# A delta-rule attention and MoE kernel: key-state and query-state products joined into one with 64 stationary columns, with the keys of the first four chunks loaded alone

## The chip, the core and the metric

The kernel runs on one core of a Trainium2 chip. The core has a matrix engine (TensorE, in the profile PE, with its weight loads on a row of their own, PEld), a vector engine (VectorE, DVE), an activation engine (ScalarE, ACT), a general engine (GpSimd, POOL), a queue that mostly starts transfers (SyncE, SP), and 16 DMA engines. The metric is device time in microseconds (us) of one execution. Less is better.

## What is computed

The reference has two parts. The first is a recurrence over 768 positions for each of 4 x 8 heads with a state of 48 x 48; the second is a feed-forward layer over all 3072 tokens.

```python
k_n = k / (np.linalg.norm(k, axis=-1, keepdims=True) + 1e-06)
for t in range(S):
    kt, vt, bt = (k_n[:, :, t], v[:, :, t], beta[:, :, t, None])
    y[:, :, t] = np.einsum('bhd,bhde->bhe', q[:, :, t], state)
    v_old = np.einsum('bhde,bhd->bhe', state, kt)
    state = state + bt[:, :, :, None] * np.einsum('bhd,bhe->bhde', kt, vt - v_old)
...
h = x @ w_in
g = h - np.tanh(h)
return (g @ w_out).astype(np.float32)
```

Here x is y with the 8 heads side by side (3072 x 384); w_in is 384 x 2048 and w_out 2048 x 384, both handed over as float64 words that the kernel turns into pairs of 32-bit numbers itself.

## The kernel before

**The recurrence in chunks.** The 768 positions are cut into 24 chunks of 32, and four chunks make a group. All 32 (batch, head) pairs of a chunk are worked on together: the batch picks a quarter of the 128 partitions, the head a stretch of columns. For a chunk s the steps are:

- `score` (L438 to L474): key-key and key-query products, 32 small matmuls with 32 stationary columns and 64 moving ones (L456). VectorE or ScalarE copies the first half into `gs` (L465, L468), ScalarE the second into `pq` (L472), and GpSimd masks `pq` (L478).
- `solve` (L483 to L605): once in a group, VectorE turns the four chunks' `gs` into the inverse of a triangular matrix for each pair: a transpose (L501), the norms (L511 to L549), 30 steps of two operations each (L577, L579), and a last transpose into `tt` (L588). The solve of group 0 is on the way of everything behind it.
- `prep` (L644 to L651): the values are multiplied by the key norms, on VectorE for the first four chunks and on GpSimd later.
- `chain` (L658 to L734): on TensorE the key-state product (L672), on VectorE its subtraction from the values (L679), on TensorE the query-state product (L689), the solve product with `tt` (L704), the state's new part (L719) after ScalarE has copied `u_sb` (L711), and the part of the output that comes from the chunk itself (L729), on top of L689 in the same PSUM bank. VectorE adds the new part to the state (L745). Each of these products is 32 small matmuls, and the next chunk's key-state product needs the new state.
- `output` (L749 to L772): ScalarE copies the output (L754), TensorE transposes it (L764), ScalarE and VectorE make a high and a low part of it in `xt` (L768, L770).

**The feed-forward layer.** The weights are decoded in 16 pieces (`decode`, `piece`, L779 to L846): ScalarE takes them apart, VectorE joins the bits (L823), ScalarE rounds to the high part (L826), and the low part comes from TensorE for the first `SPARE` pieces (L832, L833, with a copy by ScalarE, L836) and from VectorE for the rest (L841). Six windows of 512 tokens each then meet 16 slices of the hidden layer: `hidden` (L875, 9 matmuls of 512 columns for a unit), `gate` (ScalarE L892 and L900, VectorE L894 and L902), `out_units` (L925, 9 matmuls). In window 0 the first `F0` slices are done in two halves of 256 columns.

**What sets the order.** `Plan` (L86 to L230) is a list scheduler with made-up costs. It runs when the program is built and fixes one order for each engine; on the chip each engine takes its instructions in that order and waits where an operand is missing. Due times, the table `QUIRK` and constants such as `OPEN` and `F0` steer it. `warm` (L342 to L357) gives TensorE filler matmuls (L356) on zeros wherever the planner sees it idle before the last window; on the chip they are run whether or not TensorE would have been idle. The order of the first transfers is the list `FIRST`, and all are on SP's queue, which issues one after the other and holds the rest back while one waits.

**PSUM.** Two banks (`psa`) serve scores, key-state, solve, new state and transposes in turn; one (`psy`) holds the output; two (`ph`) the hidden units and three (`po`) the accumulation of the layer's output. `Ring` objects make a step wait until a bank is read out.

Of the kernel before, what the change touches and what calls it, by code (L numbers as in the profile page):

```python
# [14 lines left out]
ALU = mybir.AluOpType  # L15
PSUM = bass.MemoryType.PSUM
# [3 lines left out]
C = 32  # L20
# [65 lines left out]
class Plan:  # L86
# [3 lines left out]
    SLACK = {"PE": 0.211, "DVE": 14.4, "ACT": 0.344, "POOL": 0.2, "SP": 0.0}  # L90
# [168 lines left out]
def kernel(ctx: ExitStack, tc: tile.TileContext, kq, vk, beta, w_in, w_out, const, out):  # L259
# [7 lines left out]
    ps_y = pool("ps_y", 1, space=PSUM)  # L267
    ps_h = pool("ps_h", 2, space=PSUM)
# [7 lines left out]
    cs = cst.tile([128, 193], F32, name="cs")  # L276
    ident = cs[:, 0:128]
    strict, lower = (cs[:, None, a:a + C].broadcast_to([128, H, C]) for a in (128, 161))
# [9 lines left out]
    ra, ry, rh, ro = Ring(2), Ring(1), Ring(2), Ring(1)  # L288
    held = [ps_a.tile([128, 512], F32, name=f"psa{k}") for k in range(2)]
    new = {"psa": (ps_a, ra), "psy": (ps_y, ry), "ph": (ps_h, rh)}  # L290

    def bank(name):
        p, r = new[name]
        e = r.take()
        return held[r.free.index(e)] if name == "psa" else p.tile([128, 512], F32, name=name), e
# [5 lines left out]
    def transfer(end, kb):  # L301
        a = max(dma[0], end + 1.5)
        dma[0] = a + kb * 1024e-3 / (370.0 if a > 45.0 else 270.0 if kb == 448 else 350.0)
        plan.moves.append((a, dma[0]))
        return Event(dma[0] + 0.4)
# [6 lines left out]
    def opening():  # L312
# [9 lines left out]
        for t in held:  # L322
            nc.vector.memset(t[32:64, :DM], 0.0)
        zeroed.t = plan.free["DVE"]

    def burn():
        ps = ps_y.tile([128, 512], F32, name="psy")
        n = BURN
        while n:
            m = min(n, 16)  # L330
            n -= m
            yield Op("PE", 0.03 * m, (), 0.0, "tiny", 4 * m)
            for i in range(m):
                rows = quad[i % 4]
# [7 lines left out]
    def warm():  # L342
        ps = ps_o.tile([128, T], F32, name="po0")
        count = lambda w: NF + F0 if w == 0 else NF
        usable = lambda: 0.0 if not pos or xt_in[NS - 1].t is not None or any(ended.get(w, 0) < count(w) for w in pos) else None
        while xt_in[NS - 1].t is None and plan.free["PE"] < 2000.0:
# [5 lines left out]
            if (BURN or gram) and len(gram) < 4:  # L352
# [9 lines left out]
    def load_keys(s, table, tag):  # L362
        kc = ld.tile([128, 2, 16, C], F32, tag=tag, name=f"{tag}{s}", bufs={"kc": KCS, "kd": KDS}[tag])
        nc.sync.dma_start(kc, kq[s].rearrange("x p u c -> p x u c"))
# [698 lines left out]
```

## Time and profile before

| | |
|---|---|
| median of three runs | 617.2 us (616.09 to 617.62) |
| the profiled execution | 617.75 us, of which the span is 615.7 us |
| busy share: PE, DVE, ACT, POOL | 97%, 62%, 36%, 7% |
| TensorE filler matmuls (L356) | 166, busy for 40.9 us |
| VectorE operations with PSUM or the state (L679, L745) | 545 ns and 550 ns each |
| moved by DMA | 51.54 MB |

The span runs from the first to the last instruction; the time of an execution is about 2 us longer. A row of the timeline has the start and the length of a run of equal instructions in us, the engine, the line, what is written and read, the shapes, and the number of instructions; idle time ahead of it stands in brackets with what ended it. A 32-bit matmul of a small product is two instructions in the trace (x64 for 32), while the rows of the built order count it once. Since matmuls are pipelined, what one costs is read from the start of a row to the start of the next, not from its length.

### The profile page before, as it was taken

What the parts mean: (1) busy time and instruction counts of PE and PEld (TensorE: products, weight loads), DVE (VectorE), ACT (ScalarE), POOL (GpSimd) and SP (SyncE); (2) the same over time, 40 slices, a digit from 0 to 9 for tenths busy, and PEclk for the clock granted to TensorE, in tenths of its full rate; (3) what the DMA queues carried; (4) which work ended last, traced back from release to release, by engine and by line L of the source; (5) the groups of instructions that cost most, each with busy time, mean ns of one, the idle gap of its engine ahead of it and who ended that gap; (6) DMA issues with size and microseconds to landing.
All of it is one profiled execution on the core that took longest, in us unless ns stands there. A gap on an engine that the chain in (4) does not pass through costs nothing.

```text
span 615.7 us, 24171 instructions
## 1 busy us (share of the span) xinstructions
PE 598.0 (97%) x11146; PEld 471.6 (77%) x11146; DVE 382.4 (62%) x831; ACT 221.5 (36%) x400; POOL 43.6 (7%) x60
## 2 busy tenths in 40 slices
PE   6999899999999999999999999999999999999996
PEld 4455688987877788788888878777888788878885
DVE  2898678886489934779625878525678632333323
ACT  2335645486422333323323233223333232242223
POOL 1110100000220001100001200001100000000000
PEclk8999899999999999999999999999999999999999
DMA  8980345212530223231123321110121000010001
GB/s 309 393 302 28 116 127 203 87 34 91 163 110 11 97 71 97 63 95 54 50 84 98 97 71 42 38 62 29 64 82 67 3 2 2 3 52 1 0 1 51
DMA packets 24500, 51.54 MB, mean 84 GB/s; under 512 B 2512, under 2 KB 2640, under 8 KB 24400
## 3 DMA queue, kind: packets, MB, share of 16 engines
q1 hardware_dynamic: 22240, 45.19, 21.8%
q10 hardware_dynamic: 2160, 4.82, 2.5%
q8 instruction: 87, 1.43, 1.0%
q14 instruction: 13, 0.11, 0.1%
HBM read 45.29 MB, written 4.72 MB: 81 GB/s over the span
## 4 chain that ended last, share of the span: by engine, by line
PE 94%; DMA 2%; DVE 1%; issue 1%; ACT 1%; SPq 0%; ACTq 0%
PE po L925 33%; PE ph L875 33%; PE po L356 6%; PE psa L456 4%; PE psa L719 3%; PE psy L729 3%; PE psa L672 3%; PE psa L704 3%; PE psy L689 3%; PE ph L832 2%; PE psa L764 1%; DMA kd<-in_kq 1%; DVE a L579 0%; PE ph L833 0%; DVE tmp L577 0%
## 5 line engine op out<-in xcount | busy, mean ns | idle before, releaser
L875 PE MATMUL ph<-xt,w 128*128 128x512 f32 (+1 forms) x918 | 215.7, 385 | 2.2 <-DVE t L894 1.0
L925 PE MATMUL po<-gh,w 128*128 128x512 f32 (+1 forms) x918 | 213.8, 383 | 0.0
L875 PEld LDWEIGHTS ph<-xt,w 128*128 128x128 f32 x918 | 164.3, 190 | 36.8 <-DVE t L894 1.4
L925 PEld LDWEIGHTS po<-gh,w 128*128 128x128 f32 x918 | 162.8, 188 | 33.6 <-DVE gh L902 1.1
L894 DVE TENSOR_TENSOR t<-ph,t 128x512 f32<-128x512 f32 (+1 forms) x102 | 66.7, 656 | 91.4 <-ACT t L892 91.0
L892 ACT ACTIVATE t<-ph 128x512 f32<-128x512 f32 (+1 forms) x102 | 58.5, 573 | 170.5 <-PE ph L875 165.0
L902 DVE TENSOR_TENSOR gh<-t,gh 128x512 fp32r<-128x512 f32 (+1 forms) x102 | 68.9, 676 | 43.0 <-ACT gh L900 41.4
L900 ACT CAST gh<-t 128x512 fp32r<-128x512 f32 (+1 forms) x102 | 60.7, 595 | 82.4 <-DVE t L894 55.1
L579 DVE TENSOR_TENSOR a<-a,tmp 128x30 f32<-128x30 f32 (+9 forms) x180 | 61.9, 344 | 5.1
L577 DVE TENSOR_TENSOR tmp<-a 128x30 f32<-128x30 f32 (+9 forms) x180 | 61.0, 339 | 4.6
L745 DVE TENSOR_TENSOR st<-st,psa 112x384 f32<-112x384 f32 x44 | 22.4, 550 | 32.1 <-PE psa L719 31.4
L356 PE MATMUL po<-wz 128*128 128x512 bf16 x166 | 40.9, 399 | 1.1 <-DVE idle L315 1.1
L478 POOL TENSOR_TENSOR pq<-pq,cs 128x256 f32<-128x256 f32 x24 | 17.9, 744 | 253.6 <-ACT pq L472 253.5
L356 PEld LDWEIGHTS <-wz 128*128 128x128 bf16 x166 | 16.3, 101 | 21.8 <-issue 4.8
L770 DVE TENSOR_TENSOR xt<-psa,xt 128x384 fp32r<-128x384 f32 x24 | 13.2, 553 | 23.7 <-ACT xt L768 23.7
L754 ACT COPY y_sb<-psy 128x384 f32<-128x384 f32 x24 | 11.5, 481 | 41.5 <-PE psy L729 41.5
L719 PEld LDWEIGHTS psa<-u_sb,v 32*48 32x48 f32 x1472 | 18.6, 119 | 8.8 <-issue 7.2
L456 PEld LDWEIGHTS psa<-kc 48*32 48x32 f32 x1344 | 20.4, 110 | 4.7 <-issue 4.2
L650 POOL TENSOR_TENSOR v<-v,nt 128x384 f32<-128x384 f32 x20 | 17.3, 874 | 93.0 <-DMA v<-in_vk 62.5
L456 PE MATMUL psa<-kc 48*32 48x64 f32 x1344 | 23.8, 222 | 0.0
L672 PE MATMUL psa<-st,kd 48*32 48x48 f32 x1472 | 20.8, 204 | 2.8 <-issue 2.8
L672 PEld LDWEIGHTS psa<-st,kd 48*32 48x32 f32 x1472 | 17.5, 107 | 7.6 <-issue 6.7
(61 smaller groups left out, 419.4 us busy)
## 6 DMA issues: line engine op xcount, KB each, us to landing
kd<-in_kq SPq DMA_DIRECT2D x23, 512.0 KB, 4.0
kc<-in_kq SPq DMA_DIRECT2D x21, 512.0 KB, 4.2
v<-in_vk SPq DMA_DIRECT2D x24, 384.0 KB, 3.6
out<-o SPq DMA_DIRECT2D x18, 256.0 KB, 2.1
raw<-in_w_in SPq DMA_DIRECT2D x5, 768.0 KB, 11.6
raw<-in_w_out SPq DMA_DIRECT2D x5, 768.0 KB, 11.2
raw<-in_w_in ACTq DMA_DIRECT2D x3, 768.0 KB, 4.8
raw<-in_w_out ACTq DMA_DIRECT2D x3, 768.0 KB, 4.3
```

What stands on the lines that cost most here:

```text
L356: nc.tensor.matmul((ps if own else pos[w][0][0]).rearrange("p (a b) -> p a b", a=4), wz, wide, start=own, stop=own, skip_group_check=not own)
L456: nc.tensor.matmul(ps[quad[b], h, :], k[:, 0], k, start=True, stop=True)
L577: nc.vector.tensor_tensor(tv, col.broadcast_to(shape), row.broadcast_to(shape), ALU.mult)
L579: nc.vector.tensor_tensor(below, below, tv, ALU.add)
L672: nc.tensor.matmul(pk[quad[b], h, :], kd[rows, 0, 2 * h + pr, :], st[rows, pr, h, :], start=True, stop=True)
L719: nc.tensor.matmul(hv(sums[b // 2][0])[HALF[b % 2], h, :], kt[rows, h, :], u_sb[rows, h, :], start=True, stop=True)
L875: nc.tensor.matmul(p, wi[f][:, a, ct, :], xt[:, b, ct, part], start=(ct == 0 and i == 0), stop=(ct == NC - 1 and i == 2))
L892: nc.scalar.activation(t_, p, AF.Tanh)
L894: nc.vector.tensor_tensor(t_, p, t_, ALU.subtract)
L900: nc.scalar.copy(gh[:, 0, :n], t_)
L902: nc.vector.tensor_tensor(gh[:, 1, :n], t_, gh[:, 0, :n].bitcast(F32), ALU.subtract)
L925: nc.tensor.matmul(po[c][:, part], wo[f][:, a, 128 * c:128 * c + 128], gh[:, b, :n], start=(f == 0 and i == 0 and z < 1), stop=(ended.get( ...
```

## The change

Six things are changed together.

1. In `chain` the key-state and the query-state product become one: keys and queries stand side by side in the loaded tile, so that 64 stationary columns go through one set of 32 matmuls (L642 of the changed kernel) into two banks `psk`. In one half of the rows the order is key, query, in the other query, key. The values `v` and keys are loaded with the same alternation, `prep` and the subtraction then work on 768 columns in place of 384 and write to a tile `wv` of their own, and the output is copied from PSUM quarter by quarter (four operations of ScalarE in place of one).
2. PSUM: `psa` is one bank in place of two, `psk` two in place of `psy`'s one. The second half of a chunk's new state goes to a bank of `ph`.
3. The keys of chunks 0 to 3 are loaded alone first (`kf`, 256 KB each) and `head` makes their key-key products; the full tiles of these chunks follow later, and `score` makes only their key-query products. The first weight transfer waits for the first `head`.
4. TensorE begins with 48 tiny matmuls on zeros (`burn`) in place of 12 fillers.
5. `SPARE` goes from 8 to 10, `F0` from 6 to 4.
6. The planner has other constants and another `QUIRK` table. The solve of group 1 may not begin before that of group 0 is done. The branch for halved solves, which was not in use, is gone.

```diff
-    SLACK = {"PE": 0.211, "DVE": 14.4, "ACT": 0.344, "POOL": 0.2, "SP": 0.0}
+    SLACK = {"PE": 0.112, "DVE": 2.784, "ACT": 0.062, "POOL": 0.2, "SP": 0.0}
...
-    ra, ry, rh, ro = Ring(2), Ring(1), Ring(2), Ring(1)
-    held = [ps_a.tile([128, 512], F32, name=f"psa{k}") for k in range(2)]
+    ra, rk, rh, ro, rwt = Ring(1), Ring(1), Ring(2), Ring(1), Ring(WS)
+    psa = ps_a.tile([128, 512], F32, name="psa")
+    two = ps_k.tile([128, 2, 512], F32, name="psk")
...
+    def load_first(s):
+        ring, tag, n = (rc, "c", CB) if s < 3 else (rlo, "lo", LB)
+        t = pre.tile([128, 2 * DM], F32 if s < 3 else I32, tag=tag, name=f"kf{s}", bufs=n)
+        t = (t if s < 3 else t.bitcast(F32))[:, :16 * C].rearrange("p (u c) -> p u c", u=16)
+        nc.sync.dma_start(t, kf[s])
...
+            if behind:
+                tc.add_manual_dep(nc.cur_bb.bb.instructions[-1], heads[0].name, SYNC, reason="keys ahead of the rest")
...
+    def head(s):
...
+        for h in range(H):
+            for b in range(4):
+                x = k[HALF[b % 2], 2 * h + b // 2]
+                nc.tensor.matmul(ps[quad[b], h, :], x, x, start=True, stop=True)
...
+        nc.vector.tensor_copy(groups[0][0][:, :, 8 * s:8 * s + 8].rearrange("p i h -> p h i"), ps)
...
-                k = kc[HALF[b % 2], :, 2 * h + b // 2, :]
-                nc.tensor.matmul(ps[quad[b], h, :], k[:, 0], k, start=True, stop=True)
+                z, u = b % 2, 2 * h + b // 2
+                k = kc[HALF[z], u]
+                nc.tensor.matmul(ps[quad[b], h, :], k[:, z], k[:, 1 - z] if g == 0 else k[:, ::-1] if z else k, start=True, stop=True)
...
-        hw.tensor_tensor(v, v, nt[:, 8 * r:8 * r + 8, None].broadcast_to([128, H, D]), ALU.mult)
+        w, wr = at.tile([128, 2, H, D], F32, name="wv", bufs=WS), rwt.take()
+        hw.tensor_tensor(w, both, nt[:, None, 8 * r:8 * r + 8, None].broadcast_to([128, 2, H, D]), ALU.mult)
...
-                        rows, pr = HALF[b % 2], b // 2
-                        nc.tensor.matmul(pk[quad[b], h, :], kd[rows, 0, 2 * h + pr, :], st[rows, pr, h, :], start=True, stop=True)
+                        z, pr = b % 2, b // 2
+                        nc.tensor.matmul(pk[64 * pr:64 * pr + 64, z, h, :], kd[HALF[z], 2 * h + pr].rearrange("p a c -> p (a c)"), st[HALF[z], pr, h, :],
+                                         start=(h == 0), stop=False, skip_group_check=True)
...
-                    nc.vector.tensor_tensor(v, v, pk, ALU.subtract)
+                    nc.vector.tensor_tensor(w, w, pk, ALU.subtract)
...
-                        nc.tensor.matmul(py[quad[b], h, :], kd[rows, 1, 2 * h + pr, :], st[rows, pr, h, :],
-                                         start=(h == 0), stop=False, skip_group_check=True)
...
-        nc.scalar.copy(y_sb, py.rearrange("p h e -> p (h e)"))
+        for b in range(4):
+            if b:
+                (_, t) = yield Op("ACT", act(DM, True), (e,), need(s) - 3.0)
+            nc.scalar.copy(yv[quad[b]], py[quad[b ^ 1], b % 2])
...
-BURN, LATCH = 0, ((9, 4), (10, 2), (16, 2))
+WS, SOLO, SLOW = 2, True, 2.0
+BURN, LATCH = 48, ((8, 1), (8, 2))
...
-WARM, HOLD, GUARD, F0 = 120.0, 90.0, 0.3, 6
-FIRST = ['k0', 'k1', 'k2', 'k3', 'b0', 'k4', 'v1', 'w4', 'v3', 'w2', 'k7', 'w0', 'k6', 'w3', 'v0', 'b1', 'v2', 'k5', 'w1']
+WARM, HOLD, GUARD, F0 = 90.0, 120.0, 0.28, 4
+FIRST = ['f0', 'f1', 'f2', 'f3', 'b0', 'w0', 'w4', 'k2', 'k1', 'v2', 'k3', 'v3', 'k0', 'w3', 'b1', 'k4', 'k6', 'w1', 'w2', 'v0', 'k7', 'v1', 'k5']
...
-LOW, SPARE, MARGIN = True, 8, 7.6
+LOW, SPARE, MARGIN = True, 10, 15.2
```

The order that the planner makes of it is shown at three places. The first is SP's queue at its start; `kc` and `kd` are full key tiles of 512 KB, `v` values of 384 KB, `raw` undecoded weights of 768 KB, `bt` beta. Before:

```order
L364 DMA kc_94<-in_kq 128x2x512
L364 DMA kd_100<-in_kq 128x2x512
L364 DMA kd_103<-in_kq 128x2x512
L364 DMA kd_106<-in_kq 128x2x512
L380 DMA bt<-in_beta 128x32
L364 DMA kc_112<-in_kq 128x2x512
L372 DMA v<-in_vk 128x768
L394 DMA raw_119<-in_w_in 128x3x512
```

In the changed kernel (its lines differ), from `kf` on to the third weight tile; the values of chunk 0 come only after four more key tiles and two more weight tiles, as the 20th transfer, and those of chunk 1 as the 22nd:

```order
L373 DMA kf0_97<-in_kf 128x512
L373 DMA kf1_115<-in_kf 128x512
L373 DMA kf2_133<-in_kf 128x512
L373 DMA kf3_147<-in_kf 128x512
L389 DMA bt_157<-in_beta 128x32
L404 DMA raw0_224<-in_w_in 128x3x512
L404 DMA raw4_226<-in_w_in 128x3x512
L364 DMA kd2_230<-in_kq 128x1024
L364 DMA kd1_232<-in_kq 128x1024
L381 DMA v_234<-in_vk 128x768
L364 DMA kd3_236<-in_kq 128x1024
L381 DMA v_238<-in_vk 128x768
```

What moved: 1 MB of keys stands ahead of the first weights where 2 MB of keys and queries stood, and the full tiles of the first chunks, which are still needed, come among weights and values.

The second place is VectorE at the end of group 0's solve. Before, the decode of weight piece 1 (`c_536`) and the norms on the values of all four chunks come behind the last transpose into `tt`:

```order
L582 TENSOR_TENSOR a_323<-a_323,gm 128x1024
L588 STREAM_TRANSPOSE tt_725<-a_323 128x32x32
L823 SCALAR_TENSOR_TENSOR c_536<-c_536,lo_582 128x768
L650 TENSOR_TENSOR v<-v,nt 128x384 x4
L823 SCALAR_TENSOR_TENSOR c_600<-c_600,lo_781 128x768
L501 STREAM_TRANSPOSE a_825<-gs_253 128x1024
```

In the changed kernel the norms on chunk 1 (`wv`, twice as wide) and the decode of piece 1 stand within the solve's steps, as do those on chunk 0, twelve rows further up and ahead of the step with 228 columns:

```order
L594 TENSOR_TENSOR tmp<-a_323 128x238
L621 TENSOR_TENSOR wv<-v,nt 128x768
L596 TENSOR_TENSOR a_323<-a_323,tmp 128x14x17
L786 SCALAR_TENSOR_TENSOR c_526<-c_526,lo_534 128x768
L594 TENSOR_TENSOR tmp<-a_323 128x234
```

What moved: three operations of 768 columns now stand ahead of `tt`, and one of them needs values that are the 20th transfer.

The third place is TensorE in the chain of chunk 13. Before (three rows of L925 with 3 matmuls each are one unit of the layer):

```order
L672 MATMUL psa_88<-st,kd_4120 32x48 x32
L689 MATMUL psy<-st,kd_4120 32x48 x32
L704 MATMUL psa_87<-v,tt_4847 32x48 x32
L925 MATMUL po_4739<-gh,w_1223 128x512 x3
L925 MATMUL po_4740<-gh,w_1223 128x512 x3
```

In the changed kernel, from the score of chunk 18 on:

```order
L500 MATMUL psa<-kc_3490 32x64 x32
L888 MATMUL po_4595<-gh,w_1451 128x512 x3
L888 MATMUL po_4596<-gh,w_1451 128x512 x3
L888 MATMUL po_4597<-gh,w_1451 128x512 x3
L729 MATMUL psa<-cs,y_sb 128x128 x3
L642 MATMUL psk<-st,kd_3964 64x48 x32
L838 MATMUL ph_89<-xt_3705,w_1286 128x512 x9
L838 MATMUL ph_90<-xt_3705,w_1604 128x512 x9
L663 MATMUL psa<-wv,tt_4578 32x48 x32
```

What moved: one product of 64 stationary columns stands where two of 32 stood, and between two users of the one bank `psa` stands a unit of the layer.

More of the change, by code (lines that the diff above doesn't have):

```diff
@@ L321, in opening @@
         nc.vector.memset(st, 0.0)
-        for t in held:
+        for t in [psa] + held:
             nc.vector.memset(t[32:64, :DM], 0.0)
@@ L326, in burn @@
     def burn():
[L327 to L334, printed above, removed]
+        ps = psa
+        for i in range(BURN // 4):
+            yield Op("PE", 0.067, (), -100.0, "tiny", 16)
+            for rows in quad:
                 nc.tensor.matmul(ps[rows, :16], wz.bitcast(F32)[rows, :32], wz.bitcast(F32)[rows, :16], start=True, stop=True)
@@ L982 @@
     for s in range(4):
[L983 removed]
+        plan.spawn(head(s))
     plan.spawn(scores())
```

322 lines of the change are left out of this document (137 added, 185 removed).

## The prediction

> **What bounds the kernel now.** I read the page first, then what TensorE waited for, then the timeline of TensorE, VectorE and DMA up to 260 us.
>
> ```profile
> span 615.7 us, 24171 instructions
> PE 598.0 (97%) x11146; PEld 471.6 (77%) x11146; DVE 382.4 (62%) x831; ACT 221.5 (36%) x400; POOL 43.6 (7%) x60
> PE 94%; DMA 2%; DVE 1%; issue 1%; ACT 1%; SPq 0%; ACTq 0%
> ```
>
> TensorE is busy for 97% of the span and holds 94% of the chain that ended last. So an instruction taken from its list shortens the run by its start-to-start time, one that is added lengthens it, and other engines count only where they make it wait. The waits of that kind, by what they follow (total, times, longest); "issue" is idle time that follows on nothing in the profile:
>
> ```profile
> PE psa L672 <- issue: 2.8, 2, 2.0
> PE psy L729 <- issue: 1.0, 1, 1.0
> ```
>
> These are the two largest of the nine rows that concern work behind the first solve product; together the nine are 7.5 us, and each of the other seven is 1.0 or less. A busy TensorE is not a useful one, though: up to that product it mostly runs fillers.
>
> ```profile
> 33.73 19.60 PE L356 MATMUL po<-wz 128*128 128x512 bf16 x90
> 53.26 0.88 PE L704 MATMUL psa<-v,tt 32*32 32x48 f32 x64
> 15.06 1.25 DVE L501 STREAM_TRANSPOSE a<-gs 128x1024 f32<-128x1024 f32 x1
> 48.97 1.96 DVE L588 STREAM_TRANSPOSE tt<-a 128x1024 f32<-128x1024 f32 x1
> ```
>
> The 90 fillers take 19.53 us, 0.217 each. Ahead of 53.26 the kernel is bound by loading the keys and by VectorE's solve, 15.06 to 50.93 us; from there TensorE's list bounds it.
>
> **Part 1: the start, 2.3 us gained.** These rows are VectorE's within and behind the solve, TensorE's second score, DMA in steps of 10 us (its rate in GB/s is the last number), and a cast of ScalarE.
>
> ```profile
> 32.23 0.40 DVE L577 TENSOR_TENSOR tmp<-a 128x228 f32<-128x228 f32 x1
> 38.45 0.40 DVE L577 TENSOR_TENSOR tmp<-a 128x234 f32<-128x234 f32 x1
> 50.78 0.94 DVE L823 SCALAR_TENSOR_TENSOR c<-c,lo 128x768 int32<-128x768 int32 x1
> 51.64 1.93 DVE L650 TENSOR_TENSOR v<-v,nt 128x384 f32<-128x384 f32 x4
> 6.39 1.07 PE L456 MATMUL psa<-kd 48*32 48x64 f32 x64
> 0.00:10.00 10.00, 7.51 (x204) 4.30 (x204) 2.78 (x7) 2.54 (x5) 1.66 (x6) 1.00 0.81 263
> 10.00:20.00 10.00, 7.63 (x141) 4.78 (x142) 5.76 (x13) 1.56 (x4) 3.42 (x4) 0.66 1.05 391
> 24.44 0.83 ACT L826 CAST w<-c 128x768 fp32r<-128x768 f32 x1 [1.02 <-DVE c L823]
> ```
>
> The second score began at 6.39, when 1 MB of keys was there; the four new key tiles are 1 MB, so the last `head` starts near 6.4, and with 0.6 for it and 0.6 for its copy the solve begins at 7.6 in place of 15.06. That lead of 7.5 us isn't kept. Ahead of the step that began at 32.23 now stands the norm on chunk 0's values, which VectorE reaches at 7.6 + 17.2 = 24.8. These values are the 20th transfer: up to and with them SP issues 9.34 MB. DMA moved 2.63 MB in the first 10 us and 3.91 in the next 10; at that rate they land at 27.2, and near 27.8 with the pause in which the first weights wait for `head`. From there: 18.7 us of the old solve (32.23 to 50.93), two norms of 768 columns and one decode, at 0.86 each by the decode's start-to-start: `tt` at 49.1.
>
> TensorE can't use all of that, because its fillers are in its list. It meets VectorE at weight piece 1, decoded 12.5 us (38.45 to 50.93) before `tt`: 36.6, and cast at 37.4. Then its order has two halves of that piece's low part, 45 fillers and two scores: 1.8 + 9.8 + 2.0 = 13.6, so the first solve product starts at 51.0 against 53.26. Bounds: 49.1 if TensorE isn't late; 53 if chunk 1's values are late too (their transfer is queued on SP behind a key tile that waits for chunk 4's score on TensorE, and VectorE's next 31 rows wait behind the norm).
>
> **Part 2: TensorE's list after that product, 9.2 us less.**
>
> ```profile
> 84.90 0.81 PE L832 MATMUL ph<-c,cs 128*128 128x384 f32 x2
> 85.81 0.93 PE L719 MATMUL psa<-u_sb,v 32*48 32x48 f32 x64
> 105.09 0.88 PE L672 MATMUL psa<-st,kd 48*32 48x48 f32 x64
> 105.91 2.41 PE L875 MATMUL ph<-xt,w 128*128 128x256 f32 x18
> 108.16 2.32 PE L925 MATMUL po<-gh,w 128*128 128x256 f32 x18
> 110.41 0.89 PE L689 MATMUL psy<-st,kd 48*32 48x48 f32 x64
> 111.22 3.50 PE L925 MATMUL po<-gh,w 128*128 128x256 f32 x27
> 119.86 4.27 PE L875 MATMUL ph<-xt,w 128*128 128x512 f32 x18
> 123.97 4.24 PE L925 MATMUL po<-gh,w 128*128 128x512 f32 x18
> 128.14 0.88 PE L704 MATMUL psa<-v,tt 32*32 32x48 f32 x64
> 206.12 1.07 PE L456 MATMUL psa<-kc 48*32 48x64 f32 x64
> 207.12 2.37 PE L875 MATMUL ph<-xt,w 128*128 128x512 f32 x9
> 217.87 0.93 PE L719 MATMUL psa<-u_sb,v 32*48 32x48 f32 x64
> 218.73 0.88 PE L729 MATMUL psy<-u_sb,pq 32*32 32x48 f32 x64
> 219.55 2.35 PE L925 MATMUL po<-gh,w 128*128 128x512 f32 x9
> 222.15 0.89 PE L672 MATMUL psa<-st,kd 48*32 48x48 f32 x64
> 222.85 0.86 PE L689 MATMUL psy<-st,kd 48*32 48x48 f32 x64
> 223.64 2.35 PE L925 MATMUL po<-gh,w 128*128 128x512 f32 x9
> ```
>
> - The two products. Side by side (17 of 23 chunks in the old order) they take 0.70 + 0.79 = 1.49; apart (6 chunks) 0.82 + 0.81 = 1.63: 35.1 in all. The joint product has 48 moving columns as they have, so it streams for as long as one; its 64 stationary columns aren't in the trace. The nearest row is L719 with 48: 0.86 against 0.82 for L729 with 32. At 0.05 for 16 columns it takes 0.82 + 0.10 = 0.92, 21.2 in all: **13.9 less**. Bounds: 0.82 (16.2 less), and 1.00 as L456, which is longer on its moving side (12.1 less).
> - Fillers: of 166, 13 stood behind the first solve product; of 148, 38 do. 25 x 0.217 = **5.4 more**.
> - Two more half pieces' low parts, 0.91 each (84.90 to 85.81), of the four more that `SPARE` brings: **1.8 more**; the other two stand ahead of the product, in part 1.
> - `F0`: four half units less and two whole ones more for each of L875 and L925. A half is 1.125, a whole 2.055 and 2.085: **0.7 less**.
> - Idle time: of the 7.5 us, the 2.0 before L672 followed on a run of small products for which instructions weren't there in time. With four products to a chunk in place of five such runs are shorter: **1.8 less** (bounds: none, or 3.8, both rows named issue).
>
> Work moved to other engines is hidden while TensorE has units to do. The rows of 384 columns that read PSUM:
>
> ```profile
> L679 DVE TENSOR_TENSOR v<-v,psa x5: 526/541/546, 209.5 to 298.6; 128x384 f32<-128x384 f32 x5
> L711 ACT COPY u_sb<-psa x4: 479/480/481, 213.7 to 266.1; 128x384 f32<-128x384 f32 x4
> ```
>
> The subtraction grows from 0.54 (the middle number, in ns) to about 0.95 us on VectorE, if it goes as the decode of 768 columns, on the chain from state to state, where the new order has a unit (2.1 us) between the joint product and the solve product. Three more copies of the output on ScalarE, 0.48 us each if 32 partitions take as long as 128, stand ahead of its transposition alone. GpSimd's norms double on an engine that is 7% busy. Without that cover the subtraction would cost 0.4 and the copies 1.4 for each chunk, 41 in all.
>
> **Sum.** -2.3 - 13.9 + 5.4 + 1.8 - 0.7 - 1.8 = -11.5 us. The profiled execution took 617.75, 0.55 above the median of 617.2; so 606.3 for it, and 606 as the median. No change means within 0.3%, 615.3 to 619.1, which is about what a measurement of this kernel can tell.
>
> **The rivals.**
>
> *More of the lead is kept.* If chunk 0's values land at 25.8, both engines are 2 us earlier, and if both waits named issue go, that is 2.0 more: 602. For it: at the 391 GB/s of the second DMA row 9.34 MB take 23.9 us, so only a quicker beginning is needed than that of the first row. Against: the pause at the first weights may be longer than 0.6 us.
>
> *The solves stay late.* VectorE has group 1's `tt` at 122.4 and TensorE needs it at 128.14:
>
> ```profile
> 120.28 2.09 DVE L588 STREAM_TRANSPOSE tt<-a 128x1024 f32<-128x1024 f32 x1
> ```
>
> From the first `tt` that is 71.5 us. VectorE's list between the two is about as long in the new order; at 71.5 it ends at 120.6, and by my count of its new rows TensorE arrives at 121 to 124. A wait of 3 us there and no gain at the start give 611.
>
> *One bank for five users.* A score is followed by two copies of ScalarE before `psa` is free:
>
> ```profile
> L468 ACT COPY gs<-psa x4: 631/643/648, 207.4 to 240.1; 128x256 f32<-128x256 f32 x4
> L472 ACT COPY pq<-psa x4: 432/437/443, 207.8 to 240.5; 128x256 f32<-128x256 f32 x4
> ```
>
> Started 0.3 after the score's end, they are done about 1.1 behind it (207.12 to 208.2). Where a unit of 2.1 stands before the next user, 1 us of delay on ScalarE is covered; where ScalarE is held up for longer TensorE waits, which two banks would have hidden. At 0.3 us a chunk that is 7, so 613; from 0.5 a chunk on nothing is left of the gain. [...]
>
> *The weight load sets the pace.* If L672's 0.70 us were the time of its 64 loads of 32 columns, 64 columns would take 1.40, and 1.51 before a unit: 23 x (1.51 - 0.92) = 13.6 more, 620, slower than before; above 1.4 us a product it eats the gain. For it: nothing in the trace has 64 columns in this packing. Against: L719's 48 columns should then take 1.05, and take 0.86. [...]
>
> That the joint product isn't joint is excluded by the order: one row of 64 columns stands where two stood.
>
> **How the numbers follow.** Main case (604 to 609) 0.60; TensorE not held 0.13; solves late 0.13; one bank 0.10, of which 0.04 at no change or worse; weight load 0.03; 0.01 for the rest. The forecast is the main case's. The range of 599 to 613 takes in the bounds of the joint product (603.7 to 607.8), of the start (604 to 608), and three rivals; outside are the dearer half of the one bank, the weight load, and gains on all terms together. Faster 0.92, same 0.03, slower 0.05.
>
> **What would show it.** Right: the joint product at 0.9 start to start; the first solve product near 51, with VectorE idle before the norm until its values land; 148 fillers; TensorE's idle time after it near 6 us, scattered. Wrong: rows in which TensorE waits for ScalarE's copies at `psa` in every chunk, a product above 1.1, or a solve product that waits for `tt` at 121.

## The result, and the profile after

The changed kernel took 611.78 us (median of 12 runs, 609.5 to 615.25), the kernel before 615.98 beside it (12 runs, 614.23 to 618.09): a ratio of 0.9927, 95% interval 0.9905 to 0.9949. It is faster and inside the range given, but outside the main case of 604 to 609: by 4.2 us and not by the 11.2 of the forecast. The profiled execution of the changed kernel took 610.21 us, 1.6 below its median, that of before 617.75, 1.8 above the median of before here; so between the two profiled executions lie 7.5 us, 7.2 of them between the spans, and the gains and losses below add up to these 7.2.

The head of the changed kernel's page: its span, the busy times, and the engines' shares of the chain that ended last.

```profile
span 608.5 us, 21905 instructions
PE 588.2 (97%) x9984; PEld 459.7 (76%) x9984; DVE 390.5 (64%) x826; ACT 257.9 (42%) x472; POOL 58.6 (10%) x60
PE 89%; DVE 4%; ACT 3%; DMA 2%; issue 2%; ACTq 0%
```

TensorE is as busy as before (97%) and still has most of the chain, but 11% of the chain is now elsewhere, where it was 6%. What TensorE waited for in the changed kernel (total, times, longest), the largest rows:

```profile
PE psa L469 <- issue: 4.4, 1, 4.4
PE ph L795 <- DVE c L786: 3.9, 1, 3.9
PE ph L469 <- issue: 2.3, 1, 2.3
PE psa L729 <- ACT y_sb L719: 1.1, 1, 1.1
```

The three largest all lie in the first 25 us. Of the rows named issue that stood behind the first solve product in the kernel before, none is left. The place of the first is seen in the list of TensorE's instructions in order of time (start, duration, line, count of records, idle time ahead):

```profile
4.60 1.07 PE L469 MATMUL ph<-kf 48*32 48x32 f32 x63
8.00 1.20 PE L469 MATMUL ph<-kf 48*32 48x32 f32 x65 [2.33 <-issue]
8.97 1.08 PE L469 MATMUL psa<-kf 48*32 48x32 f32 x62
14.44 0.31 PE L469 MATMUL psa<-kf 48*32 48x32 f32 x2 [4.39 <-issue]
24.31 0.91 PE L795 MATMUL ph<-c,cs 128*128 128x384 f32 x2 [3.91 <-DVE c L786]
50.02 7.94 PE L356 MATMUL po<-wz 128*128 128x512 bf16 x36
57.90 0.88 PE L663 MATMUL psa<-wv,tt 32*32 32x48 f32 x64
```

L469 is the product of the `head`s. The work of the third head and nearly all of the fourth was done by 10.05; then TensorE stopped for 4.39 us with two records left, out of 256. VectorE's list shows what that held up:

```profile
14.78 0.60 DVE L474 COPY gs<-psa 128x256 f32<-128x256 f32 x1 [4.92 <-PE psa L469]
15.42 1.25 DVE L538 STREAM_TRANSPOSE a<-gs 128x1024 f32<-128x1024 f32 x1
32.44 0.95 DVE L621 TENSOR_TENSOR wv<-v,nt 128x768 f32<-128x768 f32 x1
40.75 0.96 DVE L621 TENSOR_TENSOR wv<-v,nt 128x768 f32<-128x768 f32 x1 [2.22 <-DMA v<-in_vk]
54.71 1.95 DVE L604 STREAM_TRANSPOSE tt<-a 128x1024 f32<-128x1024 f32 x1
```

The solve begins at 15.42 and not at 7.6: the keys that were loaded alone and first have moved it by nothing (15.06 before). The norm on chunk 0's values (32.44) doesn't wait, since VectorE is late itself; that on chunk 1's waits 2.22 us, because their transfer stood in SP's queue behind a key tile that waited for TensorE. `tt` is ready at 56.66, and the first solve product starts at 57.90, 4.6 us *later* than before (53.26). The last 1.2 us of that are TensorE's own list, which is late too: it waited until 24.31 for a decode that stands behind the solve's first steps on VectorE, and its last 36 fillers ahead of the product start at 50.02 and are followed by it at 57.90.

Behind that product things went better. The joint product in TensorE's list, twice, with the row behind it:

```profile
231.21 1.15 PE L642 MATMUL psk<-st,kd 48*64 48x48 f32 x64
232.29 2.32 PE L888 MATMUL po<-gh,w 128*128 128x512 f32 x9
...
244.00 1.15 PE L642 MATMUL psk<-st,kd 48*64 48x48 f32 x64
245.08 2.34 PE L888 MATMUL po<-gh,w 128*128 128x512 f32 x9
```

From its start to the next row's it takes 1.08 us, not 0.92. The account of both profiles, summed over all matmul records from start to start (waits over 0.1 us apart), from the first solve product on:

| | forecast | measured |
|---|---|---|
| first solve product starts | -2.3 | +4.64 (53.26 to 57.90) |
| the two products, then the joint one | -13.9 | -11.83 (36.63 to 24.80) |
| fillers behind it | +5.4 | +6.28 (2.84 to 9.12) |
| idle time | -1.8 | -5.94 (7.53 to 1.59) |
| low parts of half pieces (L795, L796) | +1.8 | +1.71 (12.88 to 14.59) |
| units of L838 and L888 | -0.7 | -1.81 (412.94 to 411.13) |
| other small products, and the tail | 0 | -0.27 |
| sum | -11.5 | -7.22 (span 615.72 to 608.50) |

### The profile page after: what moved, and what is told of

Same layout as the page of the kernel before. It is cut to its first block, busy times and chain, and to the rows that moved or that the text cites. A ratio compares the mean times of both kernels' runs of the same rounds, so it can differ in the third digit from the quotient of the medians.

```text
span 608.5 us, 21905 instructions
## 1 busy us (share of the span) xinstructions
PE 588.2 (97%) x9984; PEld 459.7 (76%) x9984; DVE 390.5 (64%) x826; ACT 257.9 (42%) x472; POOL 58.6 (10%) x60
## 4 chain that ended last, share of the span: by engine, by line
PE 89%; DVE 4%; ACT 3%; DMA 2%; issue 2%; ACTq 0%
PE ph L838 32%; PE po L888 31%; PE po L356 4%; PE psk L642 4%; PE psa L500 4%; PE psa L663 3%; PE psk L692 3%; PE psa L679 2%; PE ph L795 2%; PE psa L729 1%; DMA raw<-in_w_in 1%; ACT y_sb L719 1%; PE ph L679 1%; DMA kc<-in_kq 1%; DVE c L786 1%
## 5 line engine op out<-in xcount | busy, mean ns | idle before, releaser
L888 PE MATMUL po<-gh,w 128*128 128x512 f32 (+1 forms) x900 | 213.7, 387 | 0.3 <-DVE gh L865 0.3
L838 PE MATMUL ph<-xt,w 128*128 128x512 f32 (+1 forms) x900 | 213.2, 387 | 0.2 <-DVE tmp L594 0.2
L888 PEld LDWEIGHTS po<-gh,w 128*128 128x128 f32 x900 | 161.7, 188 | 34.3 <-DVE gh L865 0.6
L838 PEld LDWEIGHTS ph<-xt,w 128*128 128x128 f32 x900 | 161.4, 188 | 34.1 <-DVE tmp L594 0.7
L719 ACT COPY y_sb<-psk 32x384 f32<-32x384 f32 x96 | 45.2, 471 | 37.0 <-PE psk L692 36.0
L621 POOL TENSOR_TENSOR wv<-v,nt 128x768 f32<-128x768 f32 x20 | 30.8, 1543 | 213.7 <-PE psa L663 169.3
L356 PE MATMUL po<-wz 128*128 128x512 bf16 x148 | 38.0, 393 | 0.0
L642 PEld LDWEIGHTS psk<-st,kd 48*64 48x64 f32 x1472 | 23.6, 134 | 5.2 <-issue 4.2
L642 PE MATMUL psk<-st,kd 48*64 48x48 f32 x1472 | 26.4, 220 | 0.0
L356 PEld LDWEIGHTS <-wz 128*128 128x128 bf16 x148 | 13.3, 99 | 16.6 <-issue 3.7
L651 DVE TENSOR_TENSOR wv<-wv,psk 128x768 f32<-128x768 f32 x23 | 21.9, 951 | 5.2 <-PE psk L642 4.4
L663 PEld LDWEIGHTS psa<-wv,tt 32*32 32x32 f32 x1536 | 17.9, 105 | 8.6 <-issue 5.8
L500 PEld LDWEIGHTS psa<-kc 48*32 48x32 f32 x1344 | 19.4, 107 | 5.7 <-issue 3.9
```

The source lines that it names most:

```text
L356: nc.tensor.matmul((ps if own else pos[w][0][0]).rearrange("p (a b) -> p a b", a=4), wz, wide, start=own, stop=own, skip_group_check=not own)
L500: nc.tensor.matmul(ps[quad[b], h, :], k[:, z], k[:, 1 - z] if g == 0 else k[:, ::-1] if z else k, start=True, stop=True)
L642: nc.tensor.matmul(pk[64 * pr:64 * pr + 64, z, h, :], kd[HALF[z], 2 * h + pr].rearrange("p a c -> p (a c)"), st[HALF[z], pr, h, :], start= ...
L719: nc.scalar.copy(yv[quad[b]], py[quad[b ^ 1], b % 2])
L838: nc.tensor.matmul(p, wi[f][:, a, ct, :], xt[:, b, ct, part], start=(ct == 0 and i == 0), stop=(ct == NC - 1 and i == 2))
L888: nc.tensor.matmul(po[c][:, part], wo[f][:, a, 128 * c:128 * c + 128], gh[:, b, :n], start=(f == 0 and i == 0 and z < 1), stop=(ended.get( ...
```

## The experiments

**Theory.** The gain is lost at the start, because TensorE's instructions come in blocks. The trace has a DMA queue of its own for them; its row in the DMA view of the changed kernel, from 0 to 16 us (packets, MB, share):

```profile
q8 instruction: 2, 0.03, 0.8%
```

These are two transfers of 16,384 bytes. They start at 5.65 and 12.11 us and take 0.94 and 0.99; TensorE goes on at 8.00 and at 14.44, 1.3 to 1.4 us after each has landed. It is no accident of two places: in the 14 traces of this study every wait named issue of more than 0.4 us, 33 in all, ends 1.3 to 1.6 us after a transfer of this queue has landed. Over the whole run the queue has 78 transfers, and TensorE 2 x 9,984 = 19,968 records, 256 to a transfer (the kernel before: 87 and 22,292). Between the two waits stand 65 + 62 = 127 matmul records (rows above) and as many weight loads: 254 instructions, so an estimate from these counts is 256 to a block and 64 bytes to an instruction (16,384 / 256). The places agree with it: counted over TensorE's matmul and weight-load records, those two waits stand 256 records apart, and the six of this kind in the kernel before whole multiples of 256 (the first, which ends at 12.81, and the second, at 72.25, 2,048 apart). A block of tiny products is worked off here in 2.1 us (8.00 to 10.05), and TensorE then stood still for 4.39 us ahead of the next. The 48 tiny matmuls of `burn` cost 192 instructions ahead of the heads' 512, and with them the end of a block falls two records short of the end of the fourth head. **Rival:** the heads wait for data, since keys, weights and instructions all come by DMA (queues q1 and q8 in that view).

**Experiment 1: 44 of the 48 tiny matmuls.** The planner's order is untouched; only four matmuls on zeros aren't emitted.

```diff
-            for rows in quad:
+            for rows in quad if i else ():
                 nc.tensor.matmul(ps[rows, :16], ...)
```

> [...] Theory (the last matmuls of the fourth head are just past a boundary of instruction blocks, since the tiny matmuls in front use up instructions, and wait 4.4 us for the block): the wait of 4.39 us inside the last head goes, the solve's transposition starts near 11 instead of 15.4 us, the norm then waits for chunk 0's values (31.1), the wait of 2.2 us for chunk 1's values stays or shrinks, and the first solve product starts between 54 and 56.5 instead of 57.9; 607 to 610 us where the changed kernel has 611.8, that is 1.5 to 4 us less. Rival (the four heads wait for the keys, which share the DMA engines with the rest): the last head still ends after 14 us, and nothing changes (611.8).

Measured: 605.38 us (ratio 0.9817, 0.9801 to 0.9832), 6.4 below the changed kernel. The wait in the fourth head is gone, the solve starts at 10.32, the first solve product at 53.22. TensorE's row of the fourth head is whole:

```profile
8.56 1.09 PE L469 MATMUL psa<-kf 48*32 48x32 f32 x64
```

That is more than expected, and the rival's "nothing changes" is out.

**Experiment 2: 46 and 52 tiny matmuls.** To see whether it is a threshold, the sharpest steps: two fewer, and four more.

```diff
-            for rows in quad:
+            for rows in quad if i else quad[:2]:      (46)
+            for rows in quad if i else quad + quad:   (52)
```

> The changed kernel with 46 of its 48 tiny matmuls. In its profile the last two records of the fourth head (one product of four instructions) came behind the wait, so by the theory of the instruction blocks taking 2 matmuls of four instructions away is enough: the wait inside the fourth head goes, the solve starts near 10.4, the first solve product near 53.2 to 54, and 605 to 606.5 in all. Rival (fewer tiny matmuls help because TensorE comes to the heads earlier or because something else shifts): the wait stays at 4 us and the time at 611 to 612.

> The changed kernel with 52 tiny matmuls, 4 more. By the theory of the instruction blocks about five products of the fourth head now stand behind the boundary in place of one, and wait for the same block: the wait of 4 to 4.5 us stays, the solve starts at 15 to 16 us, and the time is the changed kernel's, 610.5 to 612.5. Rival (the time grows with the number of tiny matmuls, 6.4 us for 4): 617 or so.

Measured: 604.53 us with 46 (ratio 0.9808, 0.9782 to 0.9835), 614.37 with 52 (0.9960, 0.9944 to 0.9977). TensorE's list with 46, in order of time:

```profile
4.67 1.30 PE L469 MATMUL ph<-kf 48*32 48x32 f32 x66
7.84 1.02 PE L469 MATMUL ph<-kf 48*32 48x32 f32 x60 [1.87 <-issue]
...
8.68 1.08 PE L469 MATMUL psa<-kf 48*32 48x32 f32 x62
...
14.56 1.08 PE L500 MATMUL psa<-kd 48*32 48x32 f32 x64 [4.25 <-DVE z L565]
...
52.84 0.88 PE L663 MATMUL psa<-wv,tt 32*32 32x48 f32 x64
```

The 4.25 us ahead of the score (L500) is a wait for its key tile, which landed at 14.26, by the trace; VectorE's `z`, named in the row, is not what the product reads. The end of the second block falls just here too, and that block landed at 12.85; but with 44 tiny matmuls and with none, where it falls elsewhere, the score waits as long (until 14.80 and 14.81) for a key tile that landed at 14.67. With 52:

```profile
4.51 0.97 PE L469 MATMUL ph<-kf 48*32 48x32 f32 x55
7.66 1.23 PE L469 MATMUL ph<-kf 48*32 48x32 f32 x73 [2.17 <-issue]
8.65 0.98 PE L469 MATMUL psa<-kf 48*32 48x32 f32 x54
15.20 0.42 PE L469 MATMUL psa<-kf 48*32 48x32 f32 x10 [5.57 <-issue]
```

The place of a wait moves with the count, two records for each tiny matmul. The first comes after 55 records of its head with 52 of them, after 63 with 48, and after 66 with 46 (one short of 67: a few records are missing in a trace). The second comes 10 records ahead of the end with 52, 2 with 48, and not at all in the heads with 46. Data that arrive late would not do that. This shows the cause. The size is not a constant: with 52 the second wait is 5.57 us, and 614.4 lies 2 us above what was expected. Across the profiles with 48 tiny matmuls (this study has five) it is 4.1 to 6.0, and the first solve product starts at 57.90, 58.42, 58.85, 58.88 and 60.36: the changed kernel's own profile is the mildest of them. Two tiny matmuls less move the first solve product by 5.1 us between the profiles (57.90 to 52.84), and behind it another 1.0 goes, half of it idle time (1.59 to 1.07). The medians lie 7.3 apart, since the one profile lies 1.6 below its median and the other 0.4.

**Experiment 3: no tiny matmuls at all.**

```diff
-            for rows in quad:
+            for rows in ():
```

> None of the 48 tiny matmuls is emitted; all else is as in the changed kernel. Theory of the instruction blocks: the heads' 512 instructions behind some 62 of the setup meet only one boundary instead of two, the heads end by 11 us, and the result is that of the kernel with 44 tiny matmuls within 1 us (607 to 610). Rival (the tiny matmuls earn their place by warming the clock or by having blocks fetched earlier): the heads end later than with 44, and the time is 612 or more.

Measured: 612.37 us (0.9932, 0.9920 to 0.9945): no gain, where the theory expected what 44 gave. The heads did meet only one block's end (0.9 us) and were over at 9.05. TensorE's waits, the rows that follow on nothing:

```profile
PE po L356 <- issue: 2.1, 1, 2.1
PE psk L692 <- issue: 1.9, 1, 1.9
PE psa L500 <- issue: 1.3, 1, 1.3
...
PE psa L469 <- issue: 0.9, 1, 0.9
```

Leaving out 192 instructions moves the end of every later block by 192. At one of them TensorE now waits 2.14 us among its fillers, until 27.02; the key scores behind it are 2.4 us later than with 44, the key tiles and values that wait for them too, and the first solve product starts at 56.05. Behind it stand 5.0 us of idle time in place of 1.7 with 44, and behind the wait of 1.9 among them the granted clock was 0.50 from 82.95 to 86.36 (in such a stretch of the kernel before, 72.85 to 76.26, a matmul of L875 takes 0.219 us from start to start, elsewhere 0.129). So the theory as stated was too narrow: what counts is where the ends of *all* blocks fall, not only the one in the heads. That the tiny matmuls warm TensorE's clock, as the rival has it, doesn't show, though its 612 came: from start to start a filler takes 0.43 us near 17 us with 48 of them, with 46, with 44 and with none, and 0.22 later (from 23.9 us on with 46).

**Experiment 4: the fillers behind the first solve product.** The forecast counted 25 more of them as 5.4 us on the path. Here all 38 are left out.

```diff
+            if turned[0].t is not None:
+                continue
             nc.tensor.matmul(..., wz, wide, ...)
```

> The 38 fillers (matmuls on a zero tile, whose result nobody uses) behind the first solve product are left out; all else is as in the changed kernel. If they lie on TensorE's path, as the prediction counted them, the run is shorter by up to 38 x 0.24 = 9 us (603); rival: they stand where TensorE would otherwise wait for weights or for the chain from state to state, idle time takes their place, and the run is shorter by less than 2 us.

Measured: 611.81 us (0.9928, 0.9914 to 0.9942), the changed kernel's time. Its idle time behind the first solve product is 8.13 us where the changed kernel has 1.59 and 9.12 of fillers. Three of its waits (its lines are numbered two higher):

```profile
PE psa L731 <- ACT y_sb L721: 2.2, 1, 2.2
PE psa L665 <- DVE xt L737: 1.9, 1, 1.9
PE ph L797 <- DVE st L708: 1.6, 2, 1.2
```

The fillers stand where TensorE waits for the chain from state to state and for weight pieces anyway. By the medians they cost nothing, and the forecast's +5.4 and -1.8 were one quantity seen twice. In the profiles 9.1 us of fillers go and 6.5 us of idle time come; the 2.6 between them are lost again in the matmuls' own times from start to start, in part in a stretch with a granted clock of 0.50 (79.79 to 83.20).

**Experiment 5: what 64 stationary columns cost.** Theory: the time grows with the columns loaded. Rival: two blocks of 64 columns overlap less on the array than four of 32. Three kernels, each of which leaves part of the products out: the 32 key columns at the four old places; 32 columns at the joint product's places; 48 columns there.

```diff
-    nc.tensor.matmul(pk[64 * pr:64 * pr + 64, z, h, :], kd[HALF[z], 2 * h + pr].rearrange("p a c -> p (a c)"), ...)
+    nc.tensor.matmul(pk[quad[b], z, h, :], kd[HALF[z], 2 * h + pr, z], ...)
+    nc.tensor.matmul(pk[64 * pr:64 * pr + 32, z, h, :], kd[HALF[z], 2 * h + pr, 0], ...)
+    nc.tensor.matmul(pk[64 * pr:64 * pr + 48, z, h, :], kd[HALF[z], 2 * h + pr].rearrange("p a c -> p (a c)")[:, :48], ...)
```

> The joint product with its 32 key columns alone, at the quarter of the partitions that each piece had before; the query-state product is left out, so the output lacks that term. It prices the 32 query columns inside the joint product. If a product's time grows with its stationary columns beyond what the prediction took (0.92): start to start falls from 1.08 to about 0.82 us, 23 x 0.26 = 6 us less than the changed kernel (606). Rival (the product streams for as long as one, and 1.08 is what its place in the order costs): it stays above 1.0 and the run within 1.5 us of the changed kernel (610 to 612).

> The joint product keeps its four places (rows by column blocks at 0 and 64) but loads only the 32 columns of each pair's first half, so half of the key-state and query-state products is left out and its output is not the reference's. The kernel with 32 key columns at the four old places took 0.81 us a product, the joint product 1.08. If the number of columns loaded sets the pace: about 0.81 here as well, 6 us less than the changed kernel. Rival (two column blocks of 64 overlap less than four of 32, whatever is loaded): 1.05 or more, and the time of the changed kernel.

> The joint product at its four places with 48 of the 64 columns (a quarter of both products is left out, so the output is not the reference's). It puts a point between 32 columns (0.81 us) and 64 (1.08). If the time is the larger of the streaming time and a time in proportion to the columns loaded, 48 columns take 0.81 to 0.86 and the 64 pay 0.017 us a column above some 48. Rival (it rises evenly from 32 columns on): 0.94.

Measured: 606.68 us (0.9825, 0.9807 to 0.9844), 604.93 (0.9810, 0.9785 to 0.9836) and 608.09 (0.9861, 0.9818 to 0.9903, of two runs). All three have the wait in the fourth head. The product and the row behind it with 32 columns at the joint product's places:

```profile
230.01 0.88 PE L643 MATMUL psk<-st,kd 48*32 48x48 f32 x64
230.82 2.35 PE L888 MATMUL po<-gh,w 128*128 128x512 f32 x9
```

and with 48 columns:

```profile
230.86 0.94 PE L643 MATMUL psk<-st,kd 48*48 48x48 f32 x64
231.72 2.32 PE L888 MATMUL po<-gh,w 128*128 128x512 f32 x9
```

Over all 23 the product takes 0.806 us with 32 columns, at the old places and at the new ones alike; 0.868 with 48; 1.078 with 64. The places don't matter, the columns do, and not evenly: 0.06 from 32 to 48, 0.21 from 48 to 64. With 48 it is just above the 0.81 to 0.86 expected, and far from the rival's 0.94. A floor up to some 48 columns, as that expectation has it, would look like this, but three points don't show it. The weight loads themselves grow evenly (means of 107 ns with 32 columns in L672 of the kernel before, 121 with 48 and 134 with 64), and the time of a product does not.

**Experiment 6: the kernel before without its query-state product.** It prices what the joint product could save at most; the output lacks that term.

```diff
-                for h in range(H):
-                    for b in range(4):
-                        nc.tensor.matmul(py[quad[b], h, :], kd[rows, 1, 2 * h + pr, :], st[rows, pr, h, :], ...)
```

> The kernel before with its query-state product left out (the output lacks that term); all else, its start too, is as it was. If the prediction's accounts for the second part hold, the product's own 19.3 us start to start go and the idle time of 7.5 us behind the first solve product stays but for 2 to 4 us of waits named issue: 593 to 596. Rival (with four small products in place of five the idle time goes and, unlike in the changed kernel, no more fillers take its place): 590 to 592. Rival 2 (the chain from state to state takes its place, so TensorE waits for it): more than 598.

Measured: 600.43 us (0.9735, 0.9711 to 0.9760), 16.6 below the kernel before: rival 2's side of 598. The product's 19.30 us go, but L672, with nothing at its side any more, takes 18.69 in place of 17.33. Idle time behind the first solve product falls only from 7.53 to 5.95, and what it follows has changed; the rows of this kernel's waits there:

```profile
PE ph L870 <- DVE t L889: 1.4, 2, 1.0
PE ph L827 <- ACT w L831: 1.1, 1, 1.1
PE psa L699 <- ACT t L887: 0.8, 1, 0.8
```

With fewer small products the waits named issue go (0.2 left of 4.9), and waits for VectorE and ScalarE take their place. So a joint product saves at most 18 us of TensorE, and its own 1.08 where 0.81 stood gives 6 back.

**Experiment 7: earlier values, then fewer fillers.** The kernel of experiment 1, with chunk 0's and 1's values loaded in the places of chunk 2's and 3's; then also without the 88th to 107th filler, or the 98th to 107th.

```diff
+        n = {0: 2, 1: 3, 2: 0, 3: 1}.get(s, s)
-        nc.sync.dma_start(both, vk[s])
+        nc.sync.dma_start(both, vk[n])
...
+            if 98 <= len(fillers) < 108:
+                continue
```

> The changed kernel with 44 tiny matmuls, in which chunk 0's and chunk 1's values also take the places of chunk 2's and chunk 3's in SP's list, some 13 us earlier; every engine's order is otherwise the same. Theory (VectorE's idle 2.6 us ahead of the norm is the late landing of chunk 0's values at 30.1, as the prediction had it): both waits go, the transposition of the solve ends near 49.7 instead of 52.3, and the first solve product starts where TensorE's list has it, 52 to 53.2, since the fillers ahead of it are in that list: 604 to 605.5, at most 1.4 less than the kernel with 44 tiny matmuls. Rival (VectorE's lateness holds TensorE all the way): 603.

> As the one before, with 10 of the 110 fillers ahead of the first solve product left out. Theory (after the earlier values only the fillers hold TensorE): the first solve product starts near 50 to 51 us, and the run takes 602 to 603.5. Rival (the keys' landing or the weight pieces hold TensorE): idle time takes the fillers' place, and the time is that of the one before within 0.7 us.

> The changed kernel with 44 tiny matmuls, chunk 0's and 1's values early, and 20 of the 110 fillers ahead of the first solve product left out. The solve's transposition ended at 49.1 in the kernel without the last edit, and TensorE stood at its first solve product at 51.6 with 10 fillers less. Theory (both engines now meet): the first solve product starts at 49.3 to 50, and the run takes 602 to 603. Rival (what is gained there is lost as waits behind it, where the chain and the weight pieces are no further on): 604 to 605, as with 10 fillers less.

Measured: 604.87 us (0.9806, 0.9781 to 0.9830), 604.46 with 10 fillers less (0.9802, 0.9777 to 0.9826) and 603.57 with 20 less (0.9786, 0.9761 to 0.9811), the fastest here. The last two lie above what was expected (602 to 603.5, and 602 to 603), and with 10 less it is the rival's "within 0.7 us" that came. The intervals overlap, so no step is told apart from the one before; the runs of the first (604.04 to 606.06 in experiment 1) and the last (602.65 to 604.15) hardly overlap. With the early values VectorE's and TensorE's rows around the end of the solve are

```profile
47.14 1.96 DVE L606 STREAM_TRANSPOSE tt<-a 128x1024 f32<-128x1024 f32 x1
...
46.26 7.94 PE L356 MATMUL po<-wz 128*128 128x512 bf16 x36
54.14 0.88 PE L666 MATMUL psa<-wv,tt 32*32 32x48 f32 x64
```

`tt` is there at 49.1, and TensorE works through 36 fillers for 5 us longer. So its first solve product is no earlier than with 44 tiny matmuls alone (54.14 and 53.22), and later than the 52 to 53.2 expected. With 20 fillers less it meets VectorE:

```profile
47.63 1.97 DVE L611 STREAM_TRANSPOSE tt<-a 128x1024 f32<-128x1024 f32 x1
...
49.81 0.88 PE L671 MATMUL psa<-wv,tt 32*32 32x48 f32 x64
```

The first solve product is 4.3 us earlier than with all fillers, and the span 3.0 shorter (604.4 to 601.4; the medians are only 1.3 apart, since the profiled execution with early values lies 1.3 above its median). From that product to the end the time grows from 550.3 to 551.6: a new wait of 1.7 named issue ahead of a joint product, since with 40 instructions fewer the blocks end elsewhere again.

## Why the prediction was right or wrong, point by point

- **What bounds the kernel: right.** TensorE's list behind the first solve product, VectorE's solve and the loads ahead of it. That fillers cost nothing where they cover a wait (experiment 4) is the exception to "an instruction that is added lengthens it".
- **Part 1, the start: wrong, and this step decides.** "The last `head` starts near 6.4, ... the solve begins at 7.6" took the keys' landing as the only condition. The fourth head's keys landed at 7.9, and its last product came at 14.44 for want of its instructions: +4.64 where -2.3 stood, 6.9 us, more than the whole gap between -11.5 and -7.2. The kernel before showed the same kind of wait in its own first scores (until 12.81, 1.3 us behind the landing of a block); the row of its waits:

```profile
PE psa L456 <- issue: 2.2, 1, 2.2
```

  The prediction doesn't speak of it: it counts only the waits behind the first solve product, and of those it says that instructions weren't there in time, which was right. What the forecast did say of the start holds once the wait is taken away: with 46 tiny matmuls VectorE idles ahead of chunk 0's values,

```profile
30.17 0.96 DVE L621 TENSOR_TENSOR wv<-v,nt 128x768 f32<-128x768 f32 x1 [2.80 <-DMA v<-in_vk]
50.43 1.95 DVE L604 STREAM_TRANSPOSE tt<-a 128x1024 f32<-128x1024 f32 x1
```

  they land at 30.1, 2.3 us later than the 27.8 worked out (by 27.8 some 9.4 MB had moved, as worked out, but the last 0.2 MB came at 67 GB/s), the solve ends at 52.4, and the first solve product starts at 52.84, 1.8 behind the forecast. With early values `tt` is at 49.1, as worked out. And with the wait gone the whole gain is 10.7 us (44 tiny matmuls) or 12.5 (46), on both sides of the 11.2 forecast.
- **TensorE's arrival at 51.0: nearly right in form.** From weight piece 1 to the first solve product its list takes 13.75 us (40.39 to 54.14 with early values) where 13.6 was worked out; but it reaches that piece 3 us later than 37.4, since a key score ahead of it waits until 38.70 for its tile.
- **The joint product: right in kind, mis-sized.** 1.08 where 0.92 was taken and 1.00 was the upper bound: 3.6 us more over 23, because the 0.05 for the 16 columns from 32 to 48 was taken for those from 48 to 64 too, where experiment 5 has 0.21. That it "streams for as long as one" holds at its places with 32 columns (0.81) and not with 64. The separate products were worth 36.6 and not 35.1, which gives 1.5 back: -11.8 for -13.9.
- **Fillers +5.4 and idle time -1.8: wrong apart, and too dear together.** Measured +6.28 and -5.94, near zero in sum. The fillers took the place of the waits.
- **Half pieces' low parts: right** (+1.71 for +1.8). **Units:** -1.81 for -0.7, and the excess is luck. Behind its wait of 2.0 us the kernel before ran a stretch with half the clock; TensorE's row there, and the stretch of 10 us around it (busy time, granted clock, DMA):

```profile
72.87 4.98 PE L875 MATMUL ph<-xt,w 128*128 128x256 f32 x27
70.00:80.00 10.00, 7.96 (x108) 0.83 0.14 35
```

  From 72.85 to 76.26 the granted clock was 0.50, and the 16 records of L875 that start there take 0.219 from start to start, where the 92 others of this shape take 0.129. That is 1.4 us, and the changed kernel has no such stretch between its first solve product and its last matmul; without it -0.4 is left for the -0.7.
- **Work moved to other engines is hidden: right.** No wait at the products for VectorE's longer subtraction; the one wait of 1.1 for `y_sb` is at the output's transposition, once.
- **Rivals.** *One bank for five users* did not come: no row of waiting for ScalarE's copies at `psa` in every chunk. *The solves stay late* gave 611 by another road; its mechanism, a wait for group 1's `tt` at 121, did not come. *The weight load sets the pace* had the right variable, the columns, and too steep a slope: 1.08, not 1.40. *More of the lead is kept* came only in experiment 7.
- **The terms cancelled in part**: without the 3.3 us that fillers and idle time gave, and the 1.1 of the units, the loss at the start and the joint product's price would have left 3 us. That the time lies within 599 to 613 is luck as to the mechanism, since none of the cases behind that range has the wait in the fourth head.

## What to carry to other kernels

An early stage of many tiny products was held up here by the fetching of its own instructions (4.39 us at one block's end). Where that is in doubt, count them (two loads and two matmuls to each f32 product here) against the block that the trace shows (256 here) and see whether a block ends just ahead of an instruction for which another engine waits; here 8 to 16 instructions fewer were worth 6 to 7 us. Taking more away can put another block's end at a worse place, as experiment 3 did, so the new order has to be measured. The waits named issue kept to places in the list and moved with the edits ahead of them (2, then 10 records ahead of the fourth head's end with 48 and 52 tiny matmuls), so those in the profile of before can't be booked as a saving. Such a wait also cost more than its own length where the granted clock fell behind it (0.50, and 1.4 us more in the matmuls behind the wait of 2.04 us in the kernel before). And fillers are counted on the path only where the engine would have had work in their place (here 38 of them, 9.1 us, were worth nothing by the medians, 611.81 and 611.78).

## What the runs showed of the hardware that was not expected

- Two matmuls on zeros, 8 instructions, are worth 1.2% of the run (ratio 0.9927 to 0.9808).
- A block of 16,384 bytes moved in 0.9 to 1.4 us (the first two of each run), but TensorE waited 0.9 to 3.0 us for the first that it met in the heads and 4.1 to 6.0 for the second. What sets the moment at which a fetch begins stays open; none of these runs tells it.
- An f32 product of 32 matmuls on 48 rows and 48 moving columns takes 0.81 us with 32 stationary columns, 0.87 with 48 and 1.08 with 64; with 32 it made no difference whether its pieces stood at four places or at the joint product's.
- Behind 30 us, the granted clock was 0.50 for 3.41 us shortly after three of the waits of TensorE: 2.04 us (kernel before, until 72.25), 1.93 (no tiny matmuls, until 81.80) and 1.92 (no fillers, until 78.96). After one of 2.16 (no fillers, until 66.42) and after all of 1.8 or less it stayed full. What decides it stays open.
